# Three reorderings in one table: PE takes over a subtraction in four attention sections, low parts move ahead of weights' work, two FFN steps change places

## The chip, the cores and the metric

One core of a Trainium2 chip runs the whole program. The metric is device time in microseconds of one execution. The core has five engines that are fed by instruction queues of their own: TensorE (PE in the profile, with its weight loads as PEld), VectorE (DVE), ScalarE (ACT), GpSimd (POOL) and SyncE (SP), which issues the DMA transfers. In this program each engine takes its instructions in the order in which they were recorded, and an instruction that waits for another engine holds up what is recorded behind it on its own engine.

## The reference

Attention with a window of 64 positions over 8 batches, 8 heads, 576 positions and 64 channels a head, followed by a feed-forward layer (FFN) of 4608 tokens, 512 channels and 2048 hidden units with the activation relu(h)².

```python
scores = scale * np.matmul(q, k.transpose(0, 1, 3, 2))
mask = (rel >= 0) & (rel < window)            # window = 64
attn = softmax(np.where(mask, scores, -1e9))  # in the text: max, exp, sum + 1e-9
x = (attn @ v).transpose(0, 2, 1, 3).reshape(4608, 512)
h = x @ w_in;  g = np.maximum(h, 0.0) ** 2
out = (g @ w_out).astype(np.float32)
```

q, k and v are float32; w_in and w_out are float64 and reach the chip as pairs of 32-bit words.

## The kernel before, in words

**Tiles and sections.** The 4608 tokens are cut into 12 tiles of 384 (six blocks of 64). The attention of a tile is computed in three *sections*, numbered through: sections 0 to 2 give tile 0, sections 3 to 5 tile 1. Every product of the FFN is made from two fp32r halves, a high part (the value rounded) and a low part (the rest): high by high, high by low, low by high. So each section's result is split, and so are the weights and g.

**The table.** Tiles 0 and 1, all of the weights' preparation and the first steps of tile 2 are recorded by a string of tokens, `order`. A token is a letter and a number (and a last letter for the engine: `a` ACT, `d` DVE, `p` POOL). One loop goes through the tokens and records each one's instructions, and the order of the tokens is therefore the order on every engine. What comes after is recorded by a planner from costs of its own, and the change does not touch that.

The tokens of a section, with the engine and the line of the kernel before:

- `S` scores (PE, 235); `o` and `s` choose the 64 scores that count (ACT 243, DVE 253); `z`, `y` the maximum (DVE 255, POOL 257)
- `e`, `f` eight exponentials with their sums (ACT 263); `k`, `R`, `m` division by the sum (POOL 266, DVE 269, POOL 272)
- `X` four transposes into bank 2 of PSUM (PE 276); `x` puts them back in place under the masks (DVE 280)
- `V` the product with v into banks 2 and 3 (PE 298)
- `H` the high part of the result, out of banks 2 and 3 into the tile's x (ACT 313, in section 5 DVE)
- `Q` the low part: banks 2 and 3 minus the high part, into the tile's x (DVE 315). Banks 2 and 3 are free for the next section's `X` when `H` and `Q` are done.

`T`, `t` and `U`, `u` (196, 202) transpose the first batches' q and k and copy them out of PSUM.

The tokens of one slice of weights, f from 0 to 15: `a` (ACT 118), `b` (DVE 120 and 121), `c` (DVE 123), `d` (DVE 125) turn the word pairs into float32; `h` (ACT 129) takes the high part and `l` (DVE 132) the low part. `w` fetches (SP), `B` keeps the parts in DRAM for later tiles.

The tokens of one FFN step, a tile with one f: `M` twelve matmuls of 384 columns into bank 4 (PE 404); `r` relu out of bank 4 (ACT 413); `p` square (ACT 416); `g` high part (ACT 421); `G` low part (DVE 423); `O` nine matmuls of 512 columns that add to the tile's three output banks (PE 446). There is one bank for `M`, so step n+1's `M` waits for step n's `r`. `O` needs `g` for its first matmul and `G` for its third. Steps 0 to 4 are f = 0 to 4 of tile 0, then come 0 to 5 of tile 1, f = 5 of tile 0, and so on; after a tile's last step `Z` copies its output banks (ACT 455) and `W` writes them (SP).

Around the change, PE has `V3 M2 O0 O1 X4 M3 V4 O2 X5 M4 V5 O3 M5 M6` in this order, with the other tokens' work on the other engines.

## Time and profile before

| | |
|---|---|
| median of 3 runs | 851.39 us (849.84 to 851.88) |
| the profiled execution | 849.89 us |
| its span, first to last instruction | 847.6 us |
| PE busy | 830.7 us (98%), 6754 matmuls |
| DVE busy | 593.4 us (70%) |
| ACT busy | 407.1 us (48%) |
| POOL busy | 185.6 us (22%) |
| mean granted TensorE clock | 0.998 |

The profiled execution is 1.5 us under the median and 2.3 us longer than its span. A row of the timeline reads: start, length, engine, line, operation, output<-inputs, shape, count, and in brackets the idle time of the engine before it and what ended it. PE's rows overlap by some 0.15 us and the other engines' by some 0.09, because matmuls and instructions are pipelined: twelve matmuls of line 404 read 2.11 us and follow each other every 1.95 us.

### The profile page before, as it was taken

To read this page: it belongs to the slowest core of one execution; us is meant where nothing else is said; L and a number is where in the kernel's file an instruction comes from. 1 tells how busy PE (TensorE), PEld (TensorE's weight loads), DVE (VectorE), ACT (ScalarE), POOL (GpSimd) and SP (SyncE) were. 2 spreads that over 40 slices of the span, in tenths; PEclk is the share of its full clock that TensorE was granted. 3 is DMA by queue.
4 is the path that set the end of the run, shared out by engine and by line. 5 is a ranking of instruction groups with operands and counts; after the bars stand their busy time and mean duration, and the time that the engine had idled before them with its cause. 6 is when DMAs were issued, how large, how long until landed. Compare 5 with 4: busy or idle time off the path is not lost.

```text
span 847.6 us, 17705 instructions
## 1 busy us (share of the span) xinstructions
PE 830.7 (98%) x6754; PEld 762.2 (90%) x6754; DVE 593.4 (70%) x888; ACT 407.1 (48%) x1130; POOL 185.6 (22%) x237
## 2 busy tenths in 40 slices
PE   7799999999999999999999999999999999999998
PEld 6678989899999999999999999999999999999997
DVE  4999996656766867867777765788755668554553
ACT  5896774645546554544452354353455324222221
POOL 1220003204457520311230122141112131011110
PEclk9999999999999999999999999999999999999999
DMA  9979955537698884987898796999785656676411
GB/s 223 234 247 357 313 228 103 106 94 170 180 192 263 215 177 111 305 244 186 195 306 274 171 224 159 289 219 262 220 230 150 202 189 183 238 258 213 130 71 75
DMA packets 273011, 173.92 MB, mean 205 GB/s; under 512 B 190496, under 2 KB 239648, under 8 KB 270880
## 3 DMA queue, kind: packets, MB, share of 16 engines
q1 hardware_dynamic: 272928, 172.80, 73.2%
q8 instruction: 53, 0.87, 0.4%
q14 instruction: 30, 0.25, 0.1%
HBM read 138.15 MB, written 34.60 MB: 204 GB/s over the span
## 4 chain that ended last, share of the span: by engine, by line
PE 87%; DVE 8%; ACT 2%; issue 2%; DMA 0%; POOL 0%; SPq 0%; DVEq 0%; ACTq 0%; POOLq 0%
PE banks L991 29%; PE banks L910 26%; PE banks L446 11%; PE banks L404 11%; PE banks L235 4%; PE banks L298 3%; DVE a L123 2%; PE banks L276 2%; DVE a L125 1%; DVE w L132 1%; DVE a L120 1%; DVE g L423 1%; DVE a L121 1%; DVE pt L280 1%; PE banks L512 1%
## 5 line engine op out<-in xcount | busy, mean ns | idle before, releaser
L991 PE MATMUL banks<-w 128*128 128x512 f32 x1152 | 257.5, 380 | 0.0
L991 PEld LDWEIGHTS banks<-w 128*128 128x128 f32 x1152 | 215.7, 189 | 28.4
L404 PE MATMUL banks<-x,w 128*128 128x384 f32 x768 | 137.9, 329 | 1.1 <-ACT r L413 0.6
L446 PE MATMUL banks<-w,g 128*128 128x512 f32 x576 | 136.5, 382 | 1.8 <-DVE g L423 1.5
L404 PEld LDWEIGHTS banks<-x,w 128*128 128x128 f32 x768 | 126.4, 189 | 5.8 <-ACT r L413 2.3
L910 PE MATMUL banks<-x,w 128*128 128x384 f32 x768 | 130.3, 326 | 0.0
L936 POOL TENSOR_TENSOR g<-g 128x384 f32<-128x384 f32 x64 | 58.3, 913 | 324.5 <-ACT g L947 309.5
L910 PEld LDWEIGHTS banks<-x,w 128*128 128x128 f32 x768 | 125.6, 189 | 0.0
L446 PEld LDWEIGHTS banks<-w,g 128*128 128x128 f32 x576 | 106.1, 189 | 16.7 <-DVE g L423 3.6
L263 ACT ACTIVATE sel<-sel,nm 128x64 f32<-128x64 f32 x272 | 90.8, 336 | 24.5 <-DVE nm L257 23.0
L910 PE MATMUL banks<-w 128*128 128x384 f32 x576 | 100.7, 329 | 0.0
L999 DVE TENSOR_TENSOR w<-w,banks 128x512 f32<-128x512 f32 x72 | 49.5, 687 | 69.1 <-PE banks L991 69.1
L910 PEld LDWEIGHTS banks<-w 128*128 128x128 f32 x576 | 93.8, 189 | 1.9
L981 ACT CAST w<-w 128x512 fp32r<-128x512 f32 x48 | 29.8, 620 | 72.9 <-PE banks L991 72.9
L413 ACT ACTIVATE r<-banks 128x384 f32<-128x384 f32 x64 | 31.4, 490 | 69.0 <-PE banks L404 65.8
L272 POOL TENSOR_TENSOR sel<-sel,nm 128x512 f32<-128x512 f32 x33 | 36.1, 1095 | 108.8 <-ACT g L947 51.7
L981 ACT CAST w<-g 128x512 fp32r<-128x512 f32 x48 | 29.7, 620 | 62.2 <-PE banks L991 60.1
L263 ACT ACTIVATION_READ_ACCUMULATOR sel<-sel,nm 128x1 f32 x272 | 51.1, 188 | 0.0
L423 DVE TENSOR_TENSOR g<-r,g 128x384 fp32r<-128x384 f32 x64 | 37.4, 585 | 18.0 <-ACT g L421 10.2
L929 DVE SCALAR_TENSOR_TENSOR w<-w 128x384 f32<-128x384 f32 x64 | 46.9, 733 | 1.7
L924 DVE TENSOR_TENSOR w<-banks,r 128x384 f32<-128x384 f32 x64 | 38.6, 603 | 13.2 <-PE banks L910 12.9
L280 DVE TENSOR_TENSOR pt<-banks,masks 128x1024 f32<-128x1024 f32 x33 | 40.3, 1220 | 10.8 <-PE banks L276 10.8
(103 smaller groups left out, 973.7 us busy)
## 6 DMA issues: line engine op xcount, KB each, us to landing
w<-mixed SPq DMA_DIRECT2D x128, 256.0 KB, 4.9
w<-kept SPq DMA_DIRECT2D x64, 512.0 KB, 7.1
w<-kept SPq DMA_DIRECT2D x96, 256.0 KB, 5.5
kept<-w SPq DMA_DIRECT2D x16, 1024.0 KB, 8.8
vt<-in_v_dram SPq DMA_DIRECT2D x144, 64.0 KB, 3.2
w<-in_moe_w_in_dram SPq DMA_DIRECT2D x16, 512.0 KB, 7.0
w<-in_moe_w_out_dram SPq DMA_DIRECT2D x16, 512.0 KB, 8.4
raw<-in_q_dram SPq DMA_DIRECT2D x112, 72.0 KB, 3.3
```

What stands on the lines that cost most here:

```text
L263: act.activation(sels[i][:, w, hd], sels[i][:, w, hd], AF.Exp, bias=nms[i][:, n], scale=SCALE, accum_out=sums[i][:, n])
L280: dve.tensor_tensor(pts[i].rearrange("p (w n) q -> p w n q", n=2), ps_t[i][:, :, None, :].broadcast_to([P, SW, 2, P]), masks.rearrange("p ...
L404: pe.matmul(h_ps, lhsT=weights(kk, part), rhs=in_turn(x[xx][:, kk // 2, kk % 2]), start=n == 0, stop=n == 3 * NK - 1)
L423: dve.tensor_tensor(gs[n][1], rg.pop(n), gs[n][0].bitcast(F32), ALU.subtract)
L446: pe.matmul(acc(t, tb), lhsT=gg[:, ts], rhs=in_turn(weights(part)), start=f == 0 and n == 0, stop=f == NF - 1 and n == 2)
L910: pe.matmul(ps[:, :TT], lhsT=w[:, part, kk * P:(kk + 1) * P], rhs=in_turn(x[:, xx, kk]), start=n < 4 and m == 0, stop=m == 5, skip_group_c ...
L924: plan("dve", 0.6, lambda: dve.tensor_tensor(to(), ps, other(), ALU.add), [kps, ko], keys, 0, after)
L929: plan("dve", 0.57, lambda: dve.scalar_tensor_tensor(x(), x(), 0.0, x(), ALU.max, ALU.mult), [], keys)
L936: plan("pool", 0.95, lambda: pool.tensor_tensor(x(), x(), x(), ALU.mult), [], keys)
L981: plan("act", 0.62, lambda: act.copy(high(c), src()), g_keys, [kh], 0, freed("hi") if new else [])
L991: pe.matmul(ps, lhsT=gg[:, m // 2, m % 2], rhs=in_turn(wo_slot(w[m])[:, part]), start=m == 0 and n == 0, stop=m == 3 and n == 2)
L999: plan("dve", 0.72, lambda: dve.tensor_tensor(by_half(parts(tb)), by_half(parts(tb)), ordered(ps), ALU.add), [key], [kp])
```

## The change

**PE subtracts in sections 2 to 5.** A new constant, `minus`, is the identity times -1, made by one DVE instruction at the start. A new token `J` multiplies the section's high part by it, two matmuls of 256 columns that add into banks 2 and 3, which then hold result minus high part. `Q` with the ending `a` is now a plain copy of the banks to the low part on ACT, in place of DVE's subtraction. Section 5's `H` moves from DVE to ACT too. Sections 0 and 1 and those from 6 on stay as they were.

**Low parts ahead of weights' work.** `G16` is now recorded ahead of `b13`, and `G17` ahead of `d13`.

**Two steps change places.** Tile 1's last step (f = 15) was step 22 and is now step 23; tile 0's f = 7, the eighth, was step 23 and is now step 22. Tile 1's output leaves after step 23 (`Z23 W23`), and `M25` is now ahead of `S6`.

The other new arguments (`p` for POOL in `weight` and `evac`) are not used by any token.

```diff
@@ constants
     make_identity(nc, ident)
+    minus = const.tile([P, P], F32R, name="minus")
+    nc.vector.tensor_scalar(minus, ident, -1.0, None, ALU.mult)
@@ section()
                 if op == "H":
                     copier(eng or "a")(h, vals)
+                elif op == "J":
+                    for m in range(2):
+                        pe.matmul(ps[:, m, w0:w0 + nd * n].rearrange("p (d r) q -> p d (r q)", d=nd) if nd > 1 else vals[:, m],
+                                  lhsT=minus, rhs=h[:, m], start=False, stop=True, skip_group_check=True)
+                elif eng == "a":
+                    act.copy(l, vals)
                 else:
                     dve.tensor_tensor(l, vals, h.bitcast(F32), ALU.subtract)
@@ steps
             n1 += 1
     steps += [(0, f) for f in range(n0, NF)] + [(2, f) for f in range(LAG)]
+    last = steps.index((1, NF - 1))
+    steps[last:last + 2] = steps[last + 1], steps[last]
@@ order
...
-        ... V2 H2a Q2 U1 u1a d2 S4 e3 o4a k3d R3 h2 s4 M0 ...
+        ... V2 H2a U1 J2 Q2a u1a d2 S4 e3 o4a k3d R3 h2 s4 M0 ...
-        ... f4 e4 w5 w6 g1 G1 V3 H3a k4p R4 z5 Q3 h3 l3 a4 M2 r2 p2a O0 b4 O1 ...
+        ... f4 e4 w5 w6 g1 G1 V3 H3a k4p R4 z5 J3 Q3a h3 l3 a4 M2 r2 p2a O0 b4 O1 ...
-        ... V4 d4 y5p e5 f5 k5p r3 H4a p3a h4 a5 v7 v8 R5 Q4 w8 g3 O2 l4 m5p X5 ...
+        ... V4 d4 y5p e5 f5 k5p r3 H4a p3a h4 a5 v7 v8 R5 J4 Q4a w8 g3 O2 l4 m5p X5 ...
-        ... V5 w9 w10 w11 O3 r4 p4a g4 b6 H5d Q5 b5 M5 ...
+        ... V5 w9 w10 w11 O3 r4 p4a g4 b6 H5a J5 Q5a b5 M5 ...
-        B5 B6 B7 l12 a14 G15 M17 b13 O15 c13 G16 b14 O16 r17 p17a d13 g17 M18 G17 h13 c14 O17 ...
+        B5 B6 B7 l12 a14 G15 M17 G16 b13 O15 c13 b14 O16 r17 p17a g17 G17 M18 d13 h13 c14 O17 ...
-        ... M24 G23 Z22 W22 O23 r24 p24d g24 G24 S6 M25 o6a ...
+        ... M24 G23 r24 p24d g24 O23 Z23 W23 G24 M25 S6 o6a ...
```

**On PE, around section 3's product with v.** These are the scores of section 5 (`S5`), `V3`, step 2's `M` and the `O` of steps 0 and 1. Before:

```order
L235 MATMUL banks<-w 64x128 x16
L298 MATMUL banks<-w,vt 64x128 x8
L298 MATMUL banks<-w,vt 64x64 x16
L404 MATMUL banks<-x_317,w 128x384 x12
L446 MATMUL banks<-w,g 128x512 x18
L276 MATMUL banks<-ident,sel 128x128 x4
```

With the change (its lines are 2 to 8 higher, `x` is the same tile under another number):

```order
L237 MATMUL banks<-w 64x128 x16
L300 MATMUL banks<-w,vt 64x128 x8
L300 MATMUL banks<-w,vt 64x64 x16
L318 MATMUL banks<-x_629,minus 128x256 x2
L412 MATMUL banks<-x_319,w 128x384 x12
L454 MATMUL banks<-w,g 128x512 x18
L278 MATMUL banks<-ident,sel 128x128 x4
```

`J3` stands directly behind `V3`, and `M2`, `O0` and `O1` now stand behind `J3`, which reads what `H3` writes.

**On ACT, around section 3's and section 4's high parts.** The rows run from section 5's choice of scores (`o5`, 243) over section 4's eight exponentials, `g1`, `H3`, `h3`, `a4`, step 2's three and section 5's exponentials. Before:

```order
L243 COPY sel<-banks 128x512
L263 ACTIVATE sel,nm<-sel,nm 128x64 x8
L421 CAST g<-r 128x384
L313 CAST x_625<-banks 128x2x2x128
L129 CAST w<-a 128x2x512
L118 ACTIVATE a<-w 128x1024
L413 ACTIVATE r<-banks 128x384
```

With the change, and further down the rows from `H4` on:

```order
L245 COPY sel<-banks 128x512
L265 ACTIVATE sel,nm<-sel,nm 128x64 x8
L429 CAST g<-r 128x384
L315 CAST x_629<-banks 128x2x2x128
L321 CAST x_629<-banks 128x2x2x128
L131 CAST w<-a 128x2x512
L120 ACTIVATE a<-w 128x1024
```

```order
L315 CAST x_629<-banks 128x2x2x128
L424 ACTIVATE r<-r 128x384
L131 CAST w<-a 128x2x512
L120 ACTIVATE a<-w 128x1024
L321 CAST x_629<-banks 128x2x2x128
```

`Q3` (321) follows `H3` (315) at once; `Q4` stands four instructions behind `H4`, after `p3`, `h4` and `a5`.

**On DVE, around step 16's low part.** 132 is the low part of the weights of f = 11 and 12, 423 a `G`. Before:

```order
L132 TENSOR_TENSOR w<-a,w 128x2x512 x2
L423 TENSOR_TENSOR g<-r,g 128x384
L120 TENSOR_SCALAR a<-a 128x1024
L121 TENSOR_SCALAR a<-a 128x1024
L123 SCALAR_TENSOR_TENSOR a<-w,a 128x1024
L423 TENSOR_TENSOR g<-r,g 128x384
L120 TENSOR_SCALAR a<-a 128x1024
L121 TENSOR_SCALAR a<-a 128x1024
L125 SCALAR_TENSOR_TENSOR a<-w,a 128x1024
L423 TENSOR_TENSOR g<-r,g 128x384
```

With the change:

```order
L134 TENSOR_TENSOR w<-a,w 128x2x512 x2
L431 TENSOR_TENSOR g<-r,g 128x384 x2
L122 TENSOR_SCALAR a<-a 128x1024
L123 TENSOR_SCALAR a<-a 128x1024
L125 SCALAR_TENSOR_TENSOR a<-w,a 128x1024
L122 TENSOR_SCALAR a<-a 128x1024
L123 TENSOR_SCALAR a<-a 128x1024
L431 TENSOR_TENSOR g<-r,g 128x384
L127 SCALAR_TENSOR_TENSOR a<-w,a 128x1024
```

`G16` follows `G15` at once, three instructions earlier than before, and `G17` is one instruction (`d13`) earlier.

## The prediction

> **What bounds the kernel now.** First the page's shares and its chain of waits, by engine:

> ```profile
> PE 830.7 (98%) x6754; PEld 762.2 (90%) x6754; DVE 593.4 (70%) x888; ACT 407.1 (48%) x1130; POOL 185.6 (22%) x237
> PE 87%; DVE 8%; ACT 2%; issue 2%; DMA 0%; POOL 0%; SPq 0%; DVEq 0%; ACTq 0%; POOLq 0%
> ```

> PE leaves 847.6 - 830.7 = 16.9 us of the span idle, so no gain can be larger than part of that. DVE's 8% of the chain lies where the change works; the busy time by stretches (stretch, length, then PE, PEld, DVE, ACT, POOL busy with counts, granted clock, DMA share, GB/s) shows it:

> ```profile
> 36.00:62.00 26.00, 24.13 (x283) 20.25 (x287) 25.18 (x34) 24.28 (x67) 6.86 (x7) 1.00 0.82 244
> 62.00:100.00 38.00, 37.42 (x241) 34.52 (x233) 37.37 (x41) 26.63 (x40) 0.00 (x0) 1.00 1.01 324
> 100.00:118.00 18.00, 16.35 (x85) 14.41 (x85) 16.48 (x20) 12.90 (x19) 0.00 (x0) 1.00 0.98 407
> ```

> From 36 to 62 us PE, DVE and ACT are all over 92% busy: nobody has room. ACT, to which the work goes, has 1.7 us of 26 free there. From 62 to 100 PE is full. So I read the timelines of PE and ACT row by row, to see who is ahead of whom. PE:

> ```profile
> 37.51 2.58 PE L404 MATMUL banks<-x,w 128*128 128x384 f32 x12
> 40.84 0.66 PE L276 MATMUL banks<-ident,w 128*128 128x128 f32 x4 [0.36 <-POOL w L272]
> 44.30 1.08 PE L298 MATMUL banks<-w,vt 64*64 64x128 f32 x48
> 45.31 2.22 PE L404 MATMUL banks<-x,w 128*128 128x384 f32 x12
> 47.37 4.05 PE L446 MATMUL banks<-w,g 128*128 128x512 f32 x18
> 51.25 0.60 PE L276 MATMUL banks<-ident,sel 128*128 128x128 f32 x4
> 54.39 0.93 PE L298 MATMUL banks<-pt,vt 64*64 64x64 f32 x48 [0.36 <-DVE pt L280]
> 55.25 2.52 PE L446 MATMUL banks<-w,g 128*128 128x512 f32 x9
> 58.69 0.66 PE L276 MATMUL banks<-ident,sel 128*128 128x128 f32 x4 [0.92 <-POOL sel L272]
> 59.10 2.56 PE L404 MATMUL banks<-x,w 128*128 128x384 f32 x12
> 67.39 2.22 PE L404 MATMUL banks<-x,w 128*128 128x384 f32 x12 [0.58 <-ACT r L413]
> 116.96 1.78 PE L446 MATMUL banks<-w,g 128*128 128x512 f32 x7 [1.54 <-DVE g L423]
> 128.31 2.47 PE L446 MATMUL banks<-w,g 128*128 128x512 f32 x9
> ```

> These are M0, X3, V3, M2, O0 with O1, X4, V4, O2, X5, M4, M6, the rest of O16, and O19. The brackets and the stretched ones (2.47 to 2.58 where others read 2.11 to 2.22) are all that PE waits here after 36 us: 0.36 + 0.36 + 0.92 + 0.58 + 1.54 and about 0.4 four times, 5.3 us. ACT:

> ```profile
> 36.04 0.59 ACT L313 CAST x<-banks 128x512 fp32r<-128x512 f32 x1 [0.98 <-PE banks L298]
> 36.59 0.59 ACT L202 COPY w<-banks 128x512 f32<-128x512 f32 x1
> 47.70 0.50 ACT L421 CAST g<-r 128x384 fp32r<-128x384 f32 x1
> 48.10 0.58 ACT L313 CAST x<-banks 128x512 fp32r<-128x512 f32 x1
> 52.35 0.51 ACT L421 CAST g<-r 128x384 fp32r<-128x384 f32 x1
> 55.81 0.56 ACT L313 CAST x<-banks 128x512 fp32r<-128x512 f32 x1
> 58.32 1.20 ACT L118 ACTIVATE a<-w 128x1024 f32<-128x1024 f32 x1
> 62.78 0.51 ACT L421 CAST g<-r 128x384 fp32r<-128x384 f32 x1
> ```

> These are H2, u1, g1, H3, g2, H4, a5 and g4. The row that matters is H3: V3 is done at 45.38, but ACT comes to H3 only at 48.10, right behind g1, since section 5's o, eight exponentials of section 4 and g1 stand ahead of it. Before, nobody minds, because PE goes on with M2, O0 and O1.

> **The change part by part.** *What it removes:* four subtractions and one copy on DVE.

> ```profile
> L315 DVE TENSOR_TENSOR x<-banks,x 128x512 fp32r<-128x512 f32 x4 | 2.7, 670 | 0.0
> 62.79 0.69 DVE L313 CAST x<-banks 128x512 fp32r<-128x512 f32 x1
> ```

> 4 x 0.67 + 0.69 = 3.4 us as shown, about 3.0 without the overlap. *What it adds:* eight matmuls of 256 columns. The trace has no such matmul; the nearest on PE are the twelve of 384 columns in a piece of the chain of waits (start, length, what):

> ```profile
> 41.49 1.95 PE banks L404 x12
> ```

> That is 0.163 each, so two take at most 0.33 us and, by columns, 0.22, which I take; 0.9 in all. On ACT five copies of the shape of H, 0.58 each, 2.9 us in stretches where ACT has hardly any room. And four places where PE waits for H, and ACT for J. `minus` itself runs at the start, while DVE waits for PE's first transposes: nothing, and at most the 0.69 of a 128x512 row without that cover.

> *J2, +0.3.* H2 ends at 36.63, J2 runs to about 37.0, then Q2 takes ACT 0.58, so u1 starts at 37.6 instead of 36.59. The last quarter of S4 reads u1's copy, so M0 starts at 38.4, not 37.51. Against that M0 no longer waits for low parts inside (2.58 becomes 2.20) and ends near 40.5, before 40.09. X3 waits for POOL's product, which hangs on the exponentials behind u1: about 41.1 for 40.84. Bounds 0.1 (only J2's matmuls) and 0.9 (u1's delay in full).

> *J3, +3.7.* PE is through with V3 at 45.38 + 0.3 = 45.7 and now meets J3, which needs H3. H3 ends at 48.68 + 0.3 = 49.0, as ACT's row of work up to it has become late with M0 and M1. PE is idle for 3.3 to 3.5 us, then J3 takes 0.22, and M2 starts at 49.3 for 45.31: 4.0 in all, 3.7 beside J2's 0.3. Behind J3 stand M2, O0 and O1, 6.1 us of work that was ready. X4 hardly had to wait before; its input from POOL came just ahead of it:

> ```profile
> 49.74 1.04 POOL L272 TENSOR_TENSOR sel<-sel,nm 128x512 f32<-128x512 f32 x1 [0.39 <-DVE nm L269]
> ```

> Written at 50.78, used at 51.25. Now X4 follows O1 at 55.2. Bounds: 2.8 (45.38 to 48.10, were H3 as early as it was and its length hidden) and 4.1.

> *J4 and Q4, about 0.* X4's lateness goes on to DVE, whose x4 comes behind it. From there the chain is DVE's x4, c4, G2 and d4, then h4 and a5 on ACT:

> ```profile
> 53.12 1.22 DVE L280 TENSOR_TENSOR pt<-banks,masks 128x1024 f32<-128x1024 f32 x1
> ```

> x4 started at 53.12 and a5 ended at 59.52, 6.4 us. Q4 stands behind a5 and X5 needs it to free bank 2: 55.2 + 0.6 + 6.4 + 0.6 = 62.8 for 58.69, +4.1. The waits of 0.36 (V4) and 0.4 (O2) are won back and spent again on J4 (0.65 plus 0.22) and before X5. M4's inner wait of 0.36 goes: bounds -0.4 to +0.4.

> *J5 and Q5, +0.85.* J5 stands between O3 and M5, 0.22 us. M5's second matmul reads section 5's low part, which now is J5 and then 0.58 on ACT away: 0.65 more. H5 fits behind g4 (62.78) while O3 runs. Bounds 0.2 and 0.9.

> *62 to 112 us, 0.* PE is full and has nothing to win back, and M6's 0.58 stays, since M5 and M6 share a bank. DVE's 3 us go into waits for X4 and X5, and for `a`, which ACT takes behind each `r`, and so behind PE.

> *G16 and G17, -0.7.* O16 waited 1.54, and some 0.3 within, for G16, which stood behind b13 and c13:

> ```profile
> 116.36 0.54 DVE L423 TENSOR_TENSOR g<-r,g 128x384 fp32r<-128x384 f32 x1
> 119.66 1.04 ACT L129 CAST w<-a 128x1024 fp32r<-128x1024 f32 x1 [2.99 <-DVE a L125]
> 120.72 0.49 ACT L413 ACTIVATE r<-banks 128x384 f32<-128x384 f32 x1
> 122.47 2.11 PE L404 MATMUL banks<-x,w 128*128 128x384 f32 x12
> ```

> These are G16, h13, r18 and M19. Right behind G15, G16 comes in time: -1.9 or so. But d13 is then behind G17, half a microsecond later against it; h13 waits for d13, r18 stands behind h13, and M19 needs r18. It had 122.47 - 121.21 = 1.3 us to spare; PE, 1.9 us further on, finds it 0.6 late. G18, behind c14, l13 and d14 on the same DVE, is late by as much again for O18: +1.2 together. O19's 0.4 stays. Bounds -1.9 and 0.

> *Steps 22 and 23, 0.* S6 comes one `M` later, and X6 hangs on it:

> ```profile
> 146.28 1.10 PE L235 MATMUL banks<-qk 64*64 64x128 f32 x32
> 156.43 0.60 PE L276 MATMUL banks<-ident,sel 128*128 128x128 f32 x4
> ```

> In the 9 us between them M25, M26, two `O` and S7 keep PE busy, and X6 starts without a wait; without that cover it is 1.95 us. Tile 1's output leaves one step later, too.

> Together 0.3 + 3.7 + 0 + 0.85 + 0 - 0.7 + 0 = 4.15, **+4.2**.

> *The clock, +1.2.* Three stretches of 3.41 us with their granted clock:

> ```profile
> 19.44:22.85 3.41, 1.28 (x28) 0.80 (x20) 3.34 (x6) 3.19 (x17) 0.00 (x0) 1.00 0.89 194
> 22.85:26.26 3.41, 3.27 (x41) 3.16 (x42) 3.38 (x7) 2.51 (x6) 1.92 (x3) 0.50 1.04 226
> 33.09:36.50 3.41, 1.66 (x54) 1.43 (x54) 3.34 (x5) 2.43 (x11) 0.06 (x1) 1.00 0.88 265
> ```

> After a stretch in which PE was busy 1.28 of 3.41 us the clock is halved for the next 3.41; after one with 1.66 it is not. J3's idle time is as long as such a stretch. If the stretches lie anywhere against it, the nearest one misses between 0 and 1.7 us of it; as long as it misses no more than 1.28 it is as idle as the first row, 1.28 / 1.7 or three cases of four. M2 and O0 at half clock cost 3.41 / 2 = 1.7 us of a PE that is then full; three quarters of it are 1.2. Bounds 0 and 3.4 (a second one).

> [...]

> Sum: +5.4 on the profiled execution's 849.89 (span 847.6) gives 855.3. The median of the runs lies 1.5 above that execution, so 851.4 + 5.4 = **856.8 us**.

> **The rivals.** *Absorbed:* J3's 3.7 us come, but the waits listed above swallow most, because PE only arrives later where it would have waited. For it: the 5.3 us of waits are real. Against: they are waits for DVE, ACT and POOL, and x4, m5 and the `r` hang on PE's X4, M3 and M4 themselves. Price: 4.2 minus V4's, O2's, X5's, M6's and O19's waits of about 2.7, no clock term: 851.4 + 1.5 = 852.9.

> *Faster:* DVE is the chain's second engine (8% of 848 is 68 us), and 3.0 us less of it bring `x`, `b` and `G` forward, so that X5's, O2's, M4's, O16's and O19's waits (0.92, 0.4, 0.36, 1.54 and 0.3, 3.5 us) go, against 0.9 for J and Q5's 0.65: -2.0, 849.4. It decides only if H3 is written within half a microsecond of V3's end, that is if ACT reaches it by 45.9; the trace says 48.10. A variant on the same side is that a waiting J3 does not hold back M2. PE's wait of 0.36 ahead of V4 speaks against that: O2 stood behind it with g2 written at 52.86, and did not go ahead.

> *Worse:* the clock is halved twice, or ACT's 2.9 us push `r` and `a` further than reckoned: +7.5, 858.9.

> **How the numbers follow.** The forecast has 0.72, absorbed 0.14, faster 0.09, worse 0.05. Within 0.3%, 2.55 us, a measurement of this kernel can hardly be told from no change: the bounds are 848.8 and 853.9. Faster gets 0.08 (most of its case), same 0.17 (absorbed, the rest of that case, and a little of the forecast's lower end), slower 0.75. The forecast's own range is 852.9 (+1.5, J3 at its lower bound and no halved clock) to 859 (+7.6, two halved stretches). To leave out no more than two in ten the range goes down into the absorbed case: **852.3 to 859.5**.

> **What would show it.** A gap of over 3 us on PE just ahead of the matmuls from `minus` after V3, ended by ACT's H3, and M2 4 us later than 45.31 is the main step; a J3 with a gap under 1 us breaks the forecast. X5 near 62.8 with a wait for ACT's Q4 shows the second, a stretched M5 (2.7 for 2.1) the third, O16 without a wait and a new one before M19 the fourth. A clock of 0.50 around 50 to 54 shows the last term, and a full clock there takes 1.2 off. From 150 us on both traces should run in step; if PE's lateness shrinks between 62 and 112 us, the absorbed case is right.

## The result, and the profile after

The changed kernel takes **857.14 us** (median of six, 855.62 to 857.49); the kernel before took 851.09 us beside it. The ratio is 1.0069, 95% interval 1.0058 to 1.0081: some 6 us slower, where the forecast had 5.4 (856.8). A few executions far above the rest (one of the six of before took 4043.59 us) are left out of all ratios and ranges here. The profiled execution took 857.04 us with a span of 855.1 and a mean granted clock of 0.992, against 849.89, 847.6 and 0.998 before.

The page's shares and its chain of waits by engine:

```profile
PE 835.0 (98%) x6762; PEld 767.1 (90%) x6762; DVE 589.1 (69%) x884; ACT 409.3 (48%) x1135; POOL 184.0 (22%) x237
PE 87%; DVE 4%; ACT 3%; DMA 2%; SPq 2%; issue 1%; POOL 0%; DVEq 0%; ACTq 0%
```

DVE was relieved as intended: 593.4 us became 589.1, and its share of the chain fell from 8% to 4% (DMA and its queue, SPq, have 4% of it instead). Nothing was won by it, because the time went to PE: busy 4.3 us longer with only eight more matmuls, and idle for 20.1 us of the span where it was 16.9. Where PE idles is in the waits (what waited, on what, then us in all, times, longest):

```profile
PE banks L318 <- ACT x L315: 4.0, 2, 3.3
PE banks L412 <- ACT r L421: 1.3, 2, 0.7
PE banks L278 <- ACT x L321: 1.1, 1, 1.1
```

Line 318 is `J`, 315 `H`, 321 the new copy `Q`. The first and the third are new, and of the second's two, M6's 0.58 is old and M19's 0.70 new. PE's timeline has them in place; the rows answer to V3, M2, O0, X5, V5, M5 and M6 of before:

```profile
46.08 1.08 PE L300 MATMUL banks<-w,vt 64*64 64x128 f32 x48
50.50 0.80 PE L318 MATMUL banks<-x,minus 128*128 128x256 f32 x2 [3.34 <-ACT x L315]
51.10 3.45 PE L412 MATMUL banks<-x,w 128*128 128x384 f32 x12
54.38 4.05 PE L454 MATMUL banks<-w,g 128*128 128x512 f32 x18
...
65.93 0.63 PE L278 MATMUL banks<-ident,sel 128*128 128x128 f32 x4 [1.10 <-ACT x L321]
68.44 1.13 PE L300 MATMUL banks<-w,vt 64*64 64x128 f32 x48
...
71.79 0.33 PE L412 MATMUL banks<-x,w 128*128 128x384 f32 x1
72.62 2.06 PE L412 MATMUL banks<-x,w 128*128 128x384 f32 x11 [0.51 <-ACT x L321]
75.26 2.22 PE L412 MATMUL banks<-x,w 128*128 128x384 f32 x12 [0.58 <-ACT r L421]
```

The second row is J3 with its gap, behind it M2 stretched to 3.45 us; then X5 waiting for Q4's copy, V5, and M5 in two pieces, of which the second waits for Q5. ACT shows why J3 had to wait:

```profile
49.47 0.50 ACT L429 CAST g<-r 128x384 fp32r<-128x384 f32 x1
49.88 0.58 ACT L315 CAST x<-banks 128x512 fp32r<-128x512 f32 x1
```

Section 5's `o`, section 4's eight exponentials and g1 (the first row) stand ahead of H3 (the second), and ACT has no idle time among them. V3 is done at 47.16, H3 at 50.46. Stretches with their granted clock (columns as in the prediction):

```profile
33.33:40.15 6.82, 5.18 (x87) 4.36 (x87) 5.34 (x6) 4.07 (x18) 0.00 (x0) 0.50 0.86 223
46.98:50.39 3.41, 0.18 (x14) 0.04 (x4) 3.41 (x5) 3.41 (x18) 0.39 (x1) 1.00 1.08 382
50.39:53.81 3.42, 3.31 (x11) 3.31 (x12) 1.75 (x4) 2.54 (x4) 1.25 (x2) 0.50 1.01 224
```

The clock (last column but two) is halved behind J3's idle stretch, as forecast, and also from 33.33 to 40.15, which the profile of before does not have. Further on, the rows of M16, M19, M26, X6 and V6, after and then before (where the prediction has not shown them):

```profile
114.29 2.11 PE L412 MATMUL banks<-x,w 128*128 128x384 f32 x12
128.87 2.22 PE L412 MATMUL banks<-x,w 128*128 128x384 f32 x12 [0.70 <-ACT r L421]
161.51 2.11 PE L412 MATMUL banks<-x,w 128*128 128x384 f32 x12
163.80 0.66 PE L278 MATMUL banks<-ident,sel 128*128 128x128 f32 x4 [0.18 <-POOL sel L274]
165.77 1.12 PE L300 MATMUL banks<-pt,vt 64*64 64x128 f32 x40 [0.28 <-DVE pt L282]
```

```profile
61.59 1.13 PE L298 MATMUL banks<-w,vt 64*64 64x128 f32 x48
106.62 2.11 PE L404 MATMUL banks<-x,w 128*128 128x384 f32 x12
154.48 2.11 PE L404 MATMUL banks<-x,w 128*128 128x384 f32 x12
158.35 1.12 PE L298 MATMUL banks<-pt,vt 64*64 64x128 f32 x40 [0.28 <-DVE pt L280]
```

(The first row of before is V5, for the table below.) From start to start PE is later than before by 1.78 us at V3, 5.79 at M2, 7.01 at O0, 6.85 at V5, 7.87 at M6, 7.67 at M16, 7.03 at M26 and 7.42 at V6, which nearly is the whole difference of the spans (7.5).

### The profile page after: what moved, and what is told of

The parts are those of the page before. It is cut to its first block, busy times and chain, and to the rows that moved or that the text cites. A ratio compares the mean times of both kernels' runs of the same rounds, so it can differ in the third digit from the quotient of the medians.

```text
span 855.1 us, 17724 instructions
## 1 busy us (share of the span) xinstructions
PE 835.0 (98%) x6762; PEld 767.1 (90%) x6762; DVE 589.1 (69%) x884; ACT 409.3 (48%) x1135; POOL 184.0 (22%) x237
## 4 chain that ended last, share of the span: by engine, by line
PE 87%; DVE 4%; ACT 3%; DMA 2%; SPq 2%; issue 1%; POOL 0%; DVEq 0%; ACTq 0%
PE banks L1001 29%; PE banks L920 26%; PE banks L412 11%; PE banks L454 10%; PE banks L237 4%; PE banks L300 4%; PE banks L278 2%; SPq L149 1%; DMA w<-in_moe_w_out_dram 1%; DVE a L125 1%; PE banks L198 1%; DVE a L127 1%; PE banks L522 1%; ACT a L120 1%; ACT sel L265 1%
## 5 line engine op out<-in xcount | busy, mean ns | idle before, releaser
L421 ACT ACTIVATE r<-banks 128x384 f32<-128x384 f32 x64 | 31.3, 489 | 73.8 <-PE banks L412 71.8
```

## The experiments

The theory is the forecast's: the loss is J3's wait for H3, with a halved clock behind it, and the rest are small terms. The rivals: the subtraction costs what it costs wherever it stands, through ACT's additional copies; the later waits take up whatever is won or lost earlier; and, for the clock, that J3's gap has nothing to do with it.

Each run was timed against the kernel before on the same chip; that kernel's median was 850.8 to 851.1 in all of them.

**J3 left out.** DVE subtracts in section 3 as before; everything else is the whole change.

```diff
-        ... k4p R4 z5 J3 Q3a h3 l3 a4 M2 ...
+        ... k4p R4 z5 Q3 h3 l3 a4 M2 ...
```

> The change with section 3 alone as it was before: no J3, its low part subtracted on DVE. My theory (J3 holds PE up until ACT comes to H3, 3.7 us, and the idle time halves the clock once more, 1.7 us): 857.1 - 5.4, about 852, that is 0.5 to 1.5 us above the kernel before; in the trace M2 follows V3 at once and the clock is full from 41 us on. Rival (the cost is spread over all the work moved to ACT and PE, J3 is one part in four): a quarter of 6 us goes, 855.6. Rival (other waits swallow J3's in either case): 857, no change.

853.18 us (851.24 to 853.85, twelve executions), ratio 1.0026 (1.0016 to 1.0036). So J3 alone, two matmuls, is worth some 4 us of the 6. M2 follows V3 without a gap there. Three rows of PE, V3, J4 and V5:

```profile
44.86 1.08 PE L300 MATMUL banks<-w,vt 64*64 64x128 f32 x48
56.97 0.51 PE L318 MATMUL banks<-x,minus 128*128 128x256 f32 x2 [1.08 <-ACT x L315]
63.11 1.13 PE L300 MATMUL banks<-w,vt 64*64 64x128 f32 x48
```

It came out 1.2 above my 852, and the rows show where: V5 is 1.52 later than before and V3 only 0.56. Where PE is not late already, J4 and Q4 cost it 1.0 us; in the whole change, where J3's gap has made it late, it loses nothing from O0 to V5.

**J3's gap filled.** The kernel has a token `K` that lets PE multiply the identity by itself, with a result that nobody reads; eleven of these (22 rows in the trace) stand ahead of J3.

```diff
-        ... k4p R4 z5 J3 Q3a ...
+        ... k4p R4 z5 K11 J3 Q3a ...
```

> The change with eleven matmuls of the identity with itself put between V3 and J3, about 3.0 us of work for PE in the time in which it waits for H3 anyway; their result is not used. My theory (1.7 us of the loss are the halved clock after J3's idle time): no stretch of half clock from 47 to 57 us, M2 in 2.1 us in place of 3.45, and 857.1 - 1.7 = 855.4. Rival (the clock falls for another reason, or M2 at half clock is hidden by what follows): 857.1, and a half clock near 50 us or no gain from its absence.

855.37 us (853.55 to 856.00), ratio 1.0052 (1.0039 to 1.0065). J3 still waits for H3, but behind it M2 runs at full clock (1.00 from 51.02 to 54.43, after a stretch with 2.73 us of work):

```profile
46.55 1.08 PE L300 MATMUL banks<-w,vt 64*64 64x128 f32 x48
47.57 2.72 PE L522 MATMUL banks<-ident 128*128 128x128 f32 x22
50.98 0.51 PE L318 MATMUL banks<-x,minus 128*128 128x256 f32 x2 [0.69 <-ACT x L315]
51.33 2.11 PE L412 MATMUL banks<-x,w 128*128 128x384 f32 x12
```

From V3 to M2 it takes 4.78 us here, 5.02 in the change, 1.01 before. So the wait itself is 3.77 us. The halved clock adds about 0.25 to J3 and 1.2 to M2; taking it away moved the median by 1.8, and the mean granted clock went from between 0.991 and 0.996 to between 0.993 and 0.997. The intervals of the two ratios overlap, so the rows show this gain better than the times do.

**Only the second and third part.** G16 and G17 ahead of b13 and d13, the two steps exchanged, no J at all; the order up to the token `b5` is that of before.

> The change without its first part: sections 2 to 5 as before, G16 and G17 ahead of the weights' work and the two steps exchanged as in the change. My theory: these two are worth -0.7 and 0, so 850.4 (849.5 to 851.1, not to be told from the kernel before); O16 starts without a wait, M19 waits or not. Rival (the order of the G and the steps is itself harmful, since h13, r18 and S6 come later): over 852.5.

850.67 us (849.10 to 852.49), ratio 1.0000 (0.9989 to 1.0011). Together the two parts do nothing that can be measured, where the forecast had -0.7. Its profile has no gap at J3, since there is no J, and yet this stretch:

```profile
34.19:41.02 6.83, 5.56 (x87) 5.00 (x88) 6.00 (x10) 4.54 (x21) 0.00 (x0) 0.50 0.81 230
```

So the halved clock near 33 to 40 us, which the changed kernel's profile shows and that of before does not, is no work of the change's first part.

**Only the first part.** The counterpart, with J in sections 2 to 5 and the old order from `b5` on.

> The first part of the change alone: PE subtracts in sections 2 to 5, but G16, G17 and the two steps stand as before. My theory: 857.1 + 0.7 = 857.8 (857.1 to 858.5), with the wait for G16 ahead of O16 back. Rival (the first part costs less and the other two the rest): below 856.

856.41 us (855.22 to 857.27), ratio 1.0067 (1.0054 to 1.0079): 1.4 below what I expected. Half of that is the forecast's gain of 0.7 for G16 and G17, which I had taken away and which does not exist; the rest is not told from noise, for the ratio is that of the whole change (1.0069). This execution has J3's gap and no halved clock behind it:

```profile
46.52 1.08 PE L300 MATMUL banks<-w,vt 64*64 64x128 f32 x48
50.94 0.50 PE L318 MATMUL banks<-x,minus 128*128 128x256 f32 x2 [3.34 <-ACT x L315]
51.28 2.12 PE L412 MATMUL banks<-x,w 128*128 128x384 f32 x12
```

```profile
46.00:49.41 3.41, 1.60 (x76) 1.46 (x68) 3.38 (x6) 3.38 (x16) 0.00 (x0) 1.00 1.04 373
49.42:52.83 3.41, 1.89 (x12) 1.89 (x13) 2.07 (x4) 2.81 (x8) 1.49 (x3) 1.00 1.14 329
```

The gap is the same 3.34 us, but it falls on two stretches of the clock, each of which still has 1.6 to 1.9 us of work. That is the fourth case of the forecast's "three cases of four". From V3 to M2: 4.76 us, so J3's price without the clock is 3.75.

**The same subtraction, in another order.** H3 goes between ACT's exponentials, ahead of e4, and J3 behind M2.

```diff
-        ... d3 f4 e4 w5 w6 g1 G1 V3 H3a k4p R4 z5 J3 Q3a h3 l3 a4 M2 ...
+        ... d3 V3 f4 H3a M2 J3 e4 Q3a w5 w6 g1 G1 k4p R4 z5 h3 l3 a4 ...
```

> The whole change, but section 4's step is written in another order: ACT writes H3 right behind f4, ahead of e4, section 5's loads of S and g1, and PE's two matmuls J3 stand behind M2 instead of ahead of it. Every part of the work is still done. Theory (J3 costs because it meets PE before H3 is written, not because PE subtracts): the gap of 3.3 us ahead of J3 goes, with it the halved clock behind it; what stays is J2's 0.5, J5's 1.0 and e4, which ACT now does a little later: 852.5 to 853.5 us, about the run without J3. Rival (the subtraction costs its time wherever it stands, because ACT's extra copy makes section 4 late): 856 to 857 us, as the whole change.

852.77 us (851.23 to 854.01), ratio 1.0025 (1.0013 to 1.0037). The cost was the place, not the subtraction:

```profile
46.45 1.08 PE L300 MATMUL banks<-w,vt 64*64 64x128 f32 x48
47.46 2.22 PE L412 MATMUL banks<-x,w 128*128 128x384 f32 x12
49.51 0.40 PE L318 MATMUL banks<-x,minus 128*128 128x256 f32 x2
49.75 4.05 PE L454 MATMUL banks<-w,g 128*128 128x512 f32 x18
```

V3 and M2 are 1.01 apart again and J3, with no gap, takes 0.24 us from its start to the next. What is left of the first part costs about 2 us, and it still gains nothing.

**G16 and G17 alone.** The order of before, except for the second part of the change.

> The kernel before with only G16 and G17 moved ahead of b13 and d13, as in the change; the first part of x stays subtracted on DVE and the two steps stay as they were. All work is done. Theory (the gain in O16 is nearly given back by M19 and O18): PE's O16 2.11 us long instead of 3.92, a new wait of about 0.6 to 0.7 ahead of M19, O18 longer by 0.4 to 0.5, and M24 0.3 us earlier than in the kernel before, in step with M16; X6 without a wait. In all -0.3, not to be told from the kernel before by the times. The forecast's own -0.7 is the rival; it would show as M24 0.7 earlier.

849.55 us (849.23 to 852.31), ratio 0.9992 (0.9981 to 1.0002). PE's rows of M16, O15 with O16, M19, and X6:

```profile
106.43 2.11 PE L412 MATMUL banks<-x,w 128*128 128x384 f32 x12
112.27 4.34 PE L454 MATMUL banks<-w,g 128*128 128x512 f32 x18
121.17 2.22 PE L412 MATMUL banks<-x,w 128*128 128x384 f32 x12 [0.66 <-ACT r L421]
155.76 0.60 PE L278 MATMUL banks<-ident,sel 128*128 128x128 f32 x4
```

The times can't tell this from no change, but the rows can: M16, ahead of the move, is 0.19 earlier than before and X6 0.67, so the move is worth 0.5 us. O16's wait of 1.54 is gone, and M19's new one and O18's behind it take back most of that. My 0.3 was low and the forecast's 0.7 high.

**The exchange of the steps alone.**

> The kernel before with only the last step of tile 1 and tile 0's eighth change places, as in the change; everything before 140 us is the old order. All work is done. Theory (the step's lateness is not wholly covered): S6 1.95 us later, X6 with a new wait of 0.16 to 0.18 us where it had none, V6 about 0.4 us later against M24, and nothing after that: +0.4, not to be told from the kernel before by the times. Rival (the forecast: covered by nine us of other work, X6 without a wait): V6 in step with M24, 0.

849.87 us (849.28 to 852.03), ratio 0.9998 (0.9987 to 1.0009). The times can't tell; the rows of M26, X6 and V6 can:

```profile
153.94 2.11 PE L412 MATMUL banks<-x,w 128*128 128x384 f32 x12
156.22 0.66 PE L278 MATMUL banks<-ident,sel 128*128 128x128 f32 x4 [0.16 <-POOL sel L274]
158.20 1.12 PE L300 MATMUL banks<-pt,vt 64*64 64x128 f32 x40 [0.28 <-DVE pt L282]
```

This execution is 0.41 earlier than before already at O19 (127.90 for 128.31), ahead of the exchange; M26 is 0.54 earlier and V6 only 0.15: the exchange costs 0.39. X6 has a wait for POOL that it did not have, and the forecast's "X6 starts without a wait" is wrong.

**Fillers in the early gaps of before.** Five `K` ahead of V0, two behind T8, five ahead of V2.

```diff
-        ... X0 x0 V0 ... T8 z3 h1 ... f3 u2a V2 ...
+        ... X0 x0 K5 V0 ... T8 K2 z3 h1 ... f3 u2a K5 V2 ...
```

> The kernel before, plus twelve matmuls with the identity whose results nobody reads, in three early places where PE waits (ahead of V0, behind T8, ahead of V2). No other work is moved. Theory (executions of every kernel here differ by whether the clock is halved for two more stretches of 3.4 us near 33 to 40 us, after a stretch with little work on PE): with the gaps filled the clock is not halved there, nor at 23 us, the execution's mean granted clock is 0.998 or more, and all executions lie near 849.5 us, 1 to 2 below the kernel before. Rival (the two levels of the times have another cause, or the added matmuls only delay PE): 851 us or more, two levels as before.

851.31 us (849.29 to 854.49), ratio 1.0008 (0.9995 to 1.0021): no gain, and not the one level of times that I expected. The halved stretch at 23 us did go, but in the profiled execution, whose mean clock of 0.998 is that of one halved stretch, another came:

```profile
30.37:33.78 3.41, 2.85 (x25) 2.08 (x22) 3.41 (x5) 3.32 (x6) 2.22 (x2) 1.00 1.02 134
33.78:37.19 3.41, 3.41 (x38) 3.19 (x42) 3.34 (x5) 1.49 (x9) 0.00 (x0) 0.50 0.70 175
```

PE was busy for 2.85 of 3.41 us and the clock was halved all the same, and then the five fillers ahead of V2 ran at half clock (2.42 us, where they take 1.38 at full clock in the run with both below) and delayed it: V2 starts at 36.01, before at 34.84. The three executions without any halving (mean clock 1.000) took 849.29 to 849.50, no less than the best of before (849.02).

**Before, in another order.** DVE's and ACT's work from 33 to 140 us in another sequence, G16 and G17 ahead of b13 and b14 among it, with no `J` and the steps as before. Two of the places:

```diff
-        ... h4 a5 v7 v8 R5 Q4 w8 g3 O2 l4 m5p X5 x5 M4 a6 G3 V5 ...
+        ... R5 h4 v7 v8 m5p p3a g3 w8 O2 Q4 l4 X5 M4 a6 x5 a5 r4 V5 ...
-        ... l12 a14 G15 M17 b13 O15 c13 G16 b14 O16 r17 p17a d13 g17 M18 G17 h13 ...
+        ... l12 B5 a14 B6 B7 G16 M17 r17 b13 p17a b14 c13 O15 g17 O16 G17 d13 M18 h13 ...
```

> The kernel before with its written order changed from 33 to 140 us, on DVE and ACT above all: G16 and G17 ahead of b13 and b14, low parts nearer behind their r, x5 and a5 ahead of less urgent work; neither the matmuls of minus nor the change of the two steps. The same work in all. Theory (the waits that the forecast lists, 0.92 before X5, 1.54 in O16, 0.36 twice and the low parts' 0.4 each, can be had by order alone, since nothing has to be added for them): 2 us less than before, 848.5 to 850. Rival (PE's later waits take up what the earlier ones give, as with G16 and G17 in this change): 851, no difference.

850.16 us (847.73 to 850.71), ratio 0.9990 (0.9980 to 1.0000): half of what I expected. In the profiled execution X6 is 1.27 us earlier:

```profile
41.50 0.66 PE L276 MATMUL banks<-ident,w 128*128 128x128 f32 x4 [0.95 <-POOL w L272]
51.12 1.78 PE L446 MATMUL banks<-w,g 128*128 128x512 f32 x7 [0.56 <-DVE g L423]
155.16 0.60 PE L276 MATMUL banks<-ident,sel 128*128 128x128 f32 x4
```

X3's wait grew from 0.36 to 0.95 and O1 got a new one of 0.56; these took back part of what the other places gave.

**Both together.**

> The reordered kernel before together with the twelve added identity matmuls (results unused) in PE's early gaps. If both theories hold and add up: 847 to 848 us, below both kernels of the case and with a mean granted clock of 0.998 or more. If only the order counts: 849; if only the clock counts: 849.5; if neither: 851.

848.78 us (848.08 to 850.19), ratio 0.9981 (0.9972 to 0.9990). This beats both kernels: 0.2% below before, 1% below the change. Ten of its eleven executions had a mean granted clock of 0.999 or 1.000; of the 29 of before that ran beside it, none was above 0.998. It lies between the sum of the two (847 to 848) and the order alone (849). Whether the fillers gain anything here beyond the order is not shown by the times, since the two intervals overlap; the mean clocks say that no stretch was halved, unlike in the run with fillers in the old order, and why the clock held here is not settled.

**The gap filled with transposes.** PE turns the identity over 20 times ahead of J3 in place of the 22 matmuls.

```diff
-        for _ in range(n):
-            pe.matmul(banks[:, 4, :P], lhsT=ident, rhs=ident, start=True, stop=True)
+        for _ in range(20 if n == 11 else n):
+            if n == 11:
+                pe.transpose(banks[:, 4, :P], ident, ident)
+            else:
+                pe.matmul(banks[:, 4, :P], lhsT=ident, rhs=ident, start=True, stop=True)
```

> As the run that fills the gap ahead of J3, but the 22 matmuls with the identity are replaced by 20 transposes of the identity, which take PE about as long (results unused again). Theory (transposes do not count as work for the granted clock: over all profiles so far, stretches of 3.41 us in which PE was busy for at most 0.63 us with anything but transposes were followed by a halved one, however busy with transposes, and at full clock none with more than 1.14 was): the clock is halved behind J3 as in the changed kernel in about three executions of four, a clock of 0.50 near 50 to 54 us, and the time is 857 us, mean granted clock 0.996 or 0.992 in most executions. Rival (any work of PE counts): as the run with the matmuls, no halved clock behind J3, 855.4 us, mean granted clock 0.997 or 0.993.

855.53 us (854.05 to 856.44), ratio 1.0059 (1.0046 to 1.0071), mean clocks 0.993 to 0.998. My theory, that transposes do not hold the clock, falls. The stretch with nothing but the end of V3's work and the transposes, and the one behind it:

```profile
45.61:49.02 3.41, 2.39 (x25) 2.15 (x21) 3.30 (x5) 3.33 (x18) 0.27 (x1) 1.00 1.03 367
49.02:52.43 3.41, 3.41 (x20) 3.28 (x21) 1.93 (x4) 2.88 (x3) 1.25 (x2) 1.00 1.07 378
```

Full clock, and the time of the run with the matmuls. These full 128x128 transposes kept the clock as well as the matmuls did. (The trace lists both as MATMUL.)

## Why the prediction was right, point by point

The sign, the time and the place were right: 5.9 us by the ratio, 5.4 forecast. That the median came within 0.3 us of 856.8 is in part luck: several terms below are off by 0.2 to 0.4 us, most of them too low, and the sum left out a halved clock; in the profiled executions PE's lateness grew by 7.4 us where the sum had 5.4. Its terms against the trace, each as the growth of PE's lateness from one row above to the next:

| step | forecast | measured | from |
|---|---|---|---|
| J2 | +0.3 | +0.56 | V3, in the run without J3, whose mean clock is that of before (0.998), with none halved from 33.26 to 40.09 us |
| clock near 33 to 40 us | not in the sum | +1.22 | V3's 1.78 less 0.56 |
| J3 | +3.7 | +3.75 | V3 to M2 with full clock, 4.76 less 1.01 |
| clock behind J3 | +1.2 | +1.48 | O0's 7.01 less 1.78 and 3.75 |
| J4 and Q4 | 0 | -0.16 | O0 to V5 |
| J5 and Q5 | +0.85 | +1.02 | V5 to M6 |
| 62 to 112 us | 0 | -0.20 | M6 to M16 |
| G16 and G17 | -0.7 | -0.64; alone -0.48 | M16 to M26; the run with G16 and G17 only |
| exchange of the steps | 0 | +0.39 | M26 to V6, the same in the run with the exchange only |

*J2* was right in its path and a little low: in the run without J3 the last quarter of S4 waits 0.45 us for u1's copy, M0 starts at 38.72 (38.4 forecast) and has no wait inside (2.22 us long).

*J3* was right in its mechanism and to 0.05 us: PE meets J3 before ACT has come to H3. Leaving J3 out and moving H3 and J3 each took the gap away, and 4 us with it; filling it with other work did not shorten it.

*The clock* was right in that J3's idle time halved it: filling the gap kept the clock up, and the execution in which the gap fell across two stretches kept it without a filler. Its price of 1.7 us, where it occurs, was 1.48. But the three cases of four rested on 1.28 us of work as a limit, and the runs have no such limit: stretches with 2.52 and 2.85 us were followed by a halved one too (last section). That share is not shown.

*J4, Q4 and J5* were right in path and nearly in size: X5 starts at 65.93, which without the two terms of the clock (1.22 and 1.48) is 63.2 for the forecast's 62.8, and it waits for Q4. M5 takes 2.89 where the forecast had 2.7. But J4's zero holds only behind J3's gap; alone it is 1.0.

*G16 and G17* failed by a little, *the exchange* was wrong: "in the 9 us between them M25, M26, two `O` and S7 keep PE busy" counted only PE. But X6 needs POOL's product, which hangs on S6 through ACT, DVE and POOL, and that is what the trace names ahead of X6. X6 now starts 0.18 after M26's end (161.51 + 2.11), where rows without a wait overlap by some 0.16; together 0.34, and V6 adds 0.05. The 9 us of other work on PE covered most of the 1.95, not all. With G16 and G17 at -0.5 the two parts together are nothing, as the run with only these shows (1.0000).

*The way to the median* was right for a reason I did not know. By the mean clocks, the 1.5 us between the profiled execution of before and the median come from two more halved stretches, in some executions of nearly every kernel here. Of 29 timed executions of before, 14 took 849.02 to 850.39 us with a mean clock of 0.996 or more, 13 took 850.96 to 851.96 with 0.994 or 0.995, and two took 851.4 with 0.996 and 0.998. The change has two levels too: 855.62 and 855.76 with 0.996, 857.04 to 857.49 with 0.991 or 0.992. If the lower level is the one without them (it was not traced), it is 0.4 higher than the forecast's own sum for such an execution, 855.3.

The rivals: *absorbed* asked that PE's lateness shrink between 62 and 112 us, and it shrank by 0.2. *Faster* asked that J3 have no wait; the run in which it has none still lies about 2 us above before. *Worse* asked for a second halved stretch behind J3's, and there is none: the two near 33 to 40 us come without J, too.

*The range* has a slip at its lower end: J3 at its lower bound (2.8 for 3.7) and no halved clock make 4.2 - 0.9 = +3.3, that is 854.7, and not the +1.5 and 852.9 written there. The result does not depend on it.

## What to carry to other kernels

An instruction put into the queue of the engine that bounds the kernel costs what it waits for, not what it takes: J3 takes 0.24 us and cost 3.75, because its input stood behind 2.7 us of work on another in-order queue (47.16 to 49.88 above). Look up where the producer stands in its own queue at that moment, and move it, or set the consumer behind work that is ready; moved so, the same J3 cost 0.24 us. A gap on PE is paid for twice where it leads to a halved clock: filling it with work whose result is thrown away won back 1.8 of the 6 us by the medians, 1.5 by the rows.

## What the runs showed of the hardware

```profile
29.92:33.33 3.41, 2.52 (x56) 1.88 (x48) 3.41 (x6) 3.35 (x6) 2.65 (x3) 1.00 0.79 131
```

This stretch of the changed kernel, with 2.52 us of work, was followed by a halved one just as the one at 46.98 with 0.18. Before, the one at 33.09 with 1.66 us was not, nor those with 1.60 and 1.89 shown above, while 2.85 us with the fillers was. None of the halvings read here followed a wholly idle stretch; 0.18 us is the least. The 2.52 us are mostly transposes (1.38 in line 198, 0.66 in line 278) and matmuls on 64 by 64 parts (0.63 in line 300; the rows overlap), and of the 2.85 us 1.57 and 0.66 are transposes. That matmuls on 64 by 64 parts count for less does not fit the stretch at 46.00 in the run with the first part only: 1.60 us of nothing else, and no halved clock behind it. For transposes there is more: in the profiles of before, of the change and of the fillers in the early gaps, each of the five halvings follows a stretch whose busy time without the transposes' is at most 0.63 us: 0.63 at 19.44 before; 0.48 at 19.68, 0.48 at 29.92 and 0.18 at 46.98 in the change; 0.62 at 30.37 with the fillers. But the stretch at 29.68 before, with 2.64 us of work and 0.60 without the transposes', was followed by full clock, and the run with full transposes had less than 0.1 us of other work at 45.61 and kept the clock. In that run a stretch at 31.95 with 1.89 us in 54 rows was followed by a halved one, where that at 33.09 before, with 1.66 us in 54 rows, was not. A rule is not shown.

**What it costs.** Two more halved stretches near 33 to 40 us cost about 1.2 us in the profile and, by the mean clocks, part the executions of nearly every kernel here into two levels 1.5 to 2 us apart (849.0 to 850.4 and 851.0 to 852.0 us before). A comparison of two kernels that differ by less is a comparison of how often each level came up.
